# A fused convolution and gated feed-forward kernel: mask, diagonal, first weight slice and casts rearranged in its first microseconds

## The chip, the cores and the metric

The kernel runs on one core of a Trainium2 chip. The metric is the device time of one execution in microseconds (us); the median of several runs counts, lower is better. The engines are named as in the profile: PE is TensorE (PEld its weight loads), DVE is VectorE, ACT is ScalarE, POOL is GpSimd, SP is SyncE, which here only issues DMAs. A "q" behind an engine (SPq, POOLq) stands for its sequencer.

## What is computed

The input `x` has 8 sequences of 4096 tokens with 192 channels. Two steps follow each other. The first is a causal convolution of 7 taps along the sequence, one tap vector for each of 8 heads of 24 channels, with the taps normalised by a softmax. The second is a feed-forward network of 1536 hidden units whose value branch is multiplied by the rectified gate branch.

```python
w = exp(weight - max(weight, axis=-1)); w = w / (sum(w, axis=-1) + 1e-9)        # 8 heads x 7 taps
out[b, s, h, g] = sum_k w[h, k] * x_pad[b, s + k, h, g]                          # 6 zero tokens ahead
gate = maximum(out @ w_gate, 0); val = out @ w_val                               # 192 -> 1536
result = (gate * val) @ w_out                                                    # 1536 -> 192
```

All inputs and the output are float32; the kernel computes its matmuls in float16, summed in float32.

## The kernel before, in words

**Streams and units.** The 8 sequences are treated as two streams of four sequences: stream 0 (sequences 0 to 3) lies on partitions 0 to 63 and stream 1 (4 to 7) on partitions 64 to 127. A unit is 1024 tokens of both streams, 16 units in all, each in two windows of 512 tokens. The 192 channels are three chunks `c` of 64.

**Dense work.** `gate_val` (L528) runs for each window over 12 blocks `f` of 128 hidden units. Each `f` has 6 matmuls for the gate and 6 for the value (L541: three chunks, two streams, 64 rows each), then ScalarE applies the rectifier (L552) and VectorE the product (L553). Two PSUM tiles `ps` are taken for each `f` out of four, so the value tile of `f` comes free for `f + 2` when VectorE has made its product. `half_pass` (L570) projects back to 192 channels. In the first window, blocks f=0 and f=1 are treated stream by stream, and ahead of f=5 `second_block` (L394) computes the convolution of the second 512 tokens.

**The convolution.** From unit 1 on, VectorE, ScalarE and GpSimd compute the convolution of the next unit beside the dense work ("lanes"), from transposed tokens `x_r` and the tap columns `tap`. The first tokens can't wait for that, so TensorE convolves them: `conv_dense` (L352, matmul L377) multiplies token tiles `x_h` with band matrices, one for each head, which hold that head's 7 taps on diagonals. In `first_block` (L387) each of the three chunks has 40 such matmuls: 16 for the tiles `jj` = 1 to 4 of stream 0, 16 for those of stream 1 and 8 for tile `jj` = 0 (the first rows of both streams) in chunk 0; chunks 1 and 2 go tile by tile. A cast moves each chunk's result to `xc` (L392; ScalarE for c=0 and 2, VectorE for c=1).

**The start.** The order of the work is written out by hand (`manual_schedule`): each engine takes its instructions in program order. The start contains:
- the taps `wr` (L101) and, on SP's queue, stream 0's tokens as float32 into `stage`, a view of the buffer `prods` (L122), then the first rows of both streams (L138), behind a memset of their zero padding (L137);
- on GpSimd's queue a memset of `spaced` (L126), stream 1's tokens straight into `x_h` as float16 (L127), then the mask (`affine_select`, L128), which puts ones on the diagonals of `spaced`;
- the weight slices (`load_w`, L170), cut at the columns in `CUTS`: a slice's 64 rows of each chunk go to partitions 0 to 63, and `both_halves` (L177) copies them to partitions 64 to 127, on VectorE for slices 0 and 1 and on GpSimd (`pool_halves`) for the rest;
- the softmax: largest tap (L251), exponentials `ex` on ScalarE (L254), sum (L258), reciprocal (L259), the reciprocals on a diagonal, `over` (L261); `same` and `places` are sums over the mask (L238);
- TensorE's warm-up matmuls on constants (`warm_up`, L154); the matmul L272, which spreads the normalised taps over partitions; the product `diag` (L282); 14 matmuls that build the bands (L292); the evictions of the bands (`fill_band`, L329) by VectorE and ScalarE;
- the normalised taps (L304) and ten small DMAs that spread them into `tap` (L310) for the lanes;
- ScalarE's two casts of stream 0's tokens to float16 (L317) and VectorE's cast of the first rows (L335).

## Time and profile before

| what | value |
|---|---|
| median of 3 runs | 766.02 us (765.96 to 767.08) |
| span of the profiled execution, first to last instruction | 764.4 us |
| what lies around the span, by the median | 1.6 us |
| busy: PE, DVE, ACT, POOL | 99%, 92%, 79%, 50% of the span |
| granted TensorE clock in the profile's rows | 1.00 in each stage |
| first convolution matmul (L377), first dense matmul (L541) | 5.65 us, 7.66 us after the span's start |

A timeline row reads: start in us, duration in us, engine, line of the kernel, operation, what it writes and reads, how many instructions were merged into the row, and in brackets the idle time of the engine before it and what ended it. PE's matmuls overlap, so their durations contain the way through the array. A row of the DMA view names a queue, its packets, megabytes and busy share of the 16 DMA engines in a window. A row that is an issue of a DMA ends with the size and the time from the issue to the landing.

### The profile page before, as it was taken

To read this page: it belongs to the slowest core of one execution; us is meant where nothing else is said; L and a number is where in the kernel's file an instruction comes from. 1 tells how busy PE (TensorE), PEld (TensorE's weight loads), DVE (VectorE), ACT (ScalarE), POOL (GpSimd) and SP (SyncE) were. 2 spreads that over 40 slices of the span, in tenths; PEclk is the share of its full clock that TensorE was granted. 3 is DMA by queue.
4 is the path that set the end of the run, shared out by engine and by line. 5 is a ranking of instruction groups with operands and counts; after the bars stand their busy time and mean duration, and the time that the engine had idled before them with its cause. 6 is when DMAs were issued, how large, how long until landed. Compare 5 with 4: busy or idle time off the path is not lost.

```text
span 764.4 us, 25103 instructions
## 1 busy us (share of the span) xinstructions
PE 760.3 (99%) x10929; PEld 501.3 (66%) x10929; DVE 705.6 (92%) x763; ACT 600.9 (79%) x735; POOL 378.4 (50%) x244
## 2 busy tenths in 40 slices
PE   9999999999999999999999999999999999999998
PEld 5494674947649476584855848567494674947648
DVE  7998999999999999999999999999999999999891
ACT  6787887878878887887878878787787887876571
POOL 9419448093571926729175390853909347090000
PEclk9999999999999999999999999999999999999999
DMA  9969039290452805528073271722819134220202
GB/s 123 134 102 148 7 96 81 65 111 22 95 67 83 97 23 107 49 85 94 30 112 40 85 94 44 120 16 90 89 44 125 13 97 60 66 48 15 71 1 84
DMA packets 131830, 56.00 MB, mean 73 GB/s; under 512 B 96392, under 2 KB 131720, under 8 KB 131720
## 3 DMA queue, kind: packets, MB, share of 16 engines
q1 hardware_dynamic: 90680, 38.81, 23.9%
q0 software_dynamic: 40896, 15.50, 20.3%
q8 instruction: 85, 1.39, 0.8%
q14 instruction: 25, 0.20, 0.1%
q10 hardware_dynamic: 144, 0.10, 0.0%
HBM read 31.48 MB, written 25.17 MB: 74 GB/s over the span
## 4 chain that ended last, share of the span: by engine, by line
PE 99%; DVE 0%; ACT 0%; issue 0%
PE ps L541 65%; PE ps L570 32%; PE ps L619 1%; PE ps L377 0%; PE ps L154 0%; PE ps L411 0%; DVE band L329 0%; PE ps L272 0%; ACT acc L596 0%; PE ps L292 0%
## 5 line engine op out<-in xcount | busy, mean ns | idle before, releaser
L553 DVE TENSOR_TENSOR hT<-gr,ps 128x1024 f16<-128x1024 f16 (+1 forms) x386 | 469.0, 1216 | 36.6 <-ACT gr L552 9.4
L552 ACT ACTIVATE gr<-ps 128x1024 f16<-128x1024 f32 (+1 forms) x386 | 392.9, 1019 | 101.9 <-PE ps L541 99.7
L491 POOL TENSOR_TENSOR prods<-prods 128x1344 f32<-128x1344 f32 x70 | 212.4, 3034 | 290.0 <-DVE prods L487 286.7
L541 PE MATMUL ps<-xc,Wg 64*128 64x512 f16 x2304 | 311.9, 376 | 0.0
L541 PE MATMUL ps<-xc,Wv 64*128 64x512 f16 x2304 | 311.9, 376 | 0.0
L570 PEld LDWEIGHTS <-hT 64*128 64x128 f16 x5952 | 245.9, 94 | 3.7
L570 PE MATMUL ps<-Wo,hT 64*128 64x192 f16 x5952 | 248.1, 243 | 0.0
L541 PEld LDWEIGHTS <-Wv 64*128 64x128 f16 x2304 | 129.8, 94 | 118.5 <-DVE hT L553 0.3
L541 PEld LDWEIGHTS <-Wg 64*128 64x128 f16 x2304 | 112.3, 94 | 132.8 <-issue 0.2
L515 DVE SCALAR_TENSOR_TENSOR acc<-x_r,tap,acc 128x576 f32<-128x576 f16 x225 | 165.3, 813 | 0.0
L485 ACT ACTIVATE prods<-x_r,tap 128x448 f32<-128x448 f16 x222 | 130.1, 660 | 0.0
L596 ACT COPY out_s<-ps 128x768 f32<-128x768 f32 (+1 forms) x64 | 45.5, 711 | 51.3 <-PE ps L570 40.0
L203 POOL DMA_DIRECT2D x_e<-in_x_dram x58 | 47.0, 823 | 16.6 <-ACT acc L501 12.8
L465 POOL COPY x_p<-x_e 128x960 f16<-128x960 f16 (+1 forms) x58 | 50.3, 906 | 1.2 <-DMA x_e<-in_x_dram 1.1
L491 POOL TENSOR_TENSOR xc<-prods 128x1344 f16<-128x1344 f32 x14 | 42.4, 3029 | 1.1
L515 DVE SCALAR_TENSOR_TENSOR xc<-x_r,tap,acc 128x576 f16<-128x576 f16 x45 | 34.1, 813 | 0.0
L501 ACT ACTIVATE acc<-x_r,tap 128x576 f32<-128x576 f16 x45 | 31.4, 763 | 0.0
L487 DVE TENSOR_SCALAR prods<-x_r,tap 128x448 f32<-128x448 f16 x70 | 26.6, 450 | 0.0
L596 DVE COPY out_s<-ps 128x384 f32<-128x384 f32 (+1 forms) x16 | 8.7, 541 | 11.9 <-PE ps L619 9.4
L619 PE MATMUL ps<-Wo,hT 128*128 128x192 f16 x96 | 8.1, 246 | 0.0
L619 PEld LDWEIGHTS <-hT 128*128 128x128 f16 x96 | 7.9, 98 | 0.2 <-issue 0.2
L154 PE MATMUL ps<-const-bfloat16-1.0 128*128 128x512 bf16 (+1 forms) x9 | 3.9, 572 | 0.8 <-PEq L719 0.8
(54 smaller groups left out, 56.3 us busy)
## 6 DMA issues: line engine op xcount, KB each, us to landing
out_dram<-out_s SPq DMA_DIRECT2D x62, 384.0 KB, 2.7
x_e<-in_x_dram POOLq DMA_DIRECT2D x34, 192.0 KB, 7.4
x_e<-in_x_dram POOLq DMA_DIRECT2D x24, 240.0 KB, 5.6
x_r<-x_p SPq DMA_TRANSPOSE x131, 5.1
Wo<-in_moe_w_out_dram POOLq DMA_DIRECT2D x1, 576.0 KB, 7.3
x_h<-in_x_dram POOLq DMA_DIRECT2D x2, 210.0 KB, 4.8
Wg<-in_moe_w_gate_dram POOLq DMA_DIRECT2D x4, 96.0 KB, 4.1
Wv<-in_moe_w_val_dram POOLq DMA_DIRECT2D x4, 96.0 KB, 4.0
```

What stands on the lines that cost most here:

```text
L203: first = nc.gpsimd.dma_start(out=xe[:, j0 + start : j0 + n, st, :, :].rearrange("p j c r -> p j (c r)"), in_=bass.AP(tensor=x.tensor, off ...
L465: nc.gpsimd.tensor_copy(out=xp[:, j0 : j0 + n, :, st, :], in_=xe[:, j0 : j0 + n, st, :, :])
L485: engine.activation(out=out, in_=in_, func=ACTF.Copy, scale=scale)
L487: engine.tensor_scalar(out=out, in0=in_, scalar1=scale, scalar2=None, op0=ALU.mult)
L491: nc.gpsimd.tensor_tensor(out=pr[:, 0] if k < KW - 1 else xc[v + 1][:, :, LDVE:UNIT], in0=pr[:, 0], in1=pr[:, k], op=ALU.add,)
L501: nc.scalar.activation(out=accs[v][:, c, :], in_=shifted(v, c, 0, 0), func=ACTF.Copy, scale=tap[:, c, 0:1],)
L515: nc.vector.scalar_tensor_tensor(out=xc[v][:, c, 0:LDVE] if k == KW - 1 else acc[:, c, :], in0=shifted(v, c, k, 0), scalar=tap[:, c, k : k ...
L541: nc.tensor.matmul(out=pss[i][:, st, :], lhsT=W[64 * st : 64 * st + 64, c, 128 * f : 128 * (f + 1)], rhs=xcb[64 * st : 64 * st + 64, c, WI ...
L552: nc.scalar.activation(out=gr[:, sts], in_=pss[0][:, sts], func=ACTF.Relu)
L553: nc.vector.tensor_tensor(out=h[:, f, sts], in0=gr[:, sts], in1=pss[1][:, sts], op=ALU.mult)
L570: mm = nc.tensor.matmul(out=outs[q], lhsT=h[64 * r : 64 * r + 64, f, st, 128 * q : 128 * (q + 1)], rhs=Wo[64 * r : 64 * r + 64, f, :], sta ...
L596: one(out=dst[:, step * j : step * j + step], in_=src[:, step * j : step * j + step])
```

## The change

- The mask (`affine_select`) is filled ahead of GpSimd's first DMA issue, which loads stream 1.
- The memset and the transfer of the first rows move from ahead of the warm-up to behind the largest-tap reduction.
- The diagonal of reciprocals is made in two operations instead of three. `ex` gets one more row. It holds 2^127 beside the diagonal and 0 on it, so that a sum over taps for each of 8 columns is the softmax's sum on the diagonal and huge elsewhere; its reciprocal is then `over`. The row is filled from the mask ahead of the largest-tap reduction, and `same` moves there too. The sum `sm`, its reciprocal and the normalised taps for `tap` are now made by VectorE behind its last band, with the ten small DMAs behind them.
- The last warm-up matmul of the first seven (256 columns) goes.
- The weight slices are cut every 256 columns, so slice 0 has 256 columns instead of 128 and serves f=0 and f=1. VectorE copies its first 128 columns where it copied slice 0, and the second 128 behind the first block, ahead of slice 1.
- The cast of stream 0's tokens is shared: ScalarE casts channels 0 to 63 of all four tiles and channels 64 to 191 of tiles 1 and 2; GpSimd casts these channels of tiles 3 and 4, between its weight issues.
- In the first block VectorE takes the cast of chunk 2 instead of chunk 1.

```diff
     nc.gpsimd.memset(spaced[:], 0.0)
-    nc.gpsimd.dma_start(out=xts[0][0:SUB, 1:GSUB, 1, :], in_=body(1))
     nc.gpsimd.affine_select(
...
     )
-    nc.vector.memset(stage(0, 32, 0, 2, 0, 1), 0.0)
-    nc.sync.dma_start(
-        out=stage(PAD, FIRST, 0, 2, 0, 1),
...
-    )
+    nc.gpsimd.dma_start(out=xts[0][0:SUB, 1:GSUB, 1, :], in_=body(1))
...
-    warm_up(512, 512, 512, 512, 512, 512, 256)
+    warm_up(512, 512, 512, 512, 512, 512)
...
-    CUTS = [0, 128, 384, 640, 896, 1152, DFF]
+    CUTS = [0, 256, 512, 768, 1024, 1280, DFF]
...
-    def both_halves(copy, s, dst):
-        cols = slice(CUTS[s], CUTS[s + 1])
+    def both_halves(copy, s, dst, half=None):
+        lo, hi = CUTS[s], CUTS[s + 1]
+        cols = slice(lo, hi) if half is None else slice(lo + 128 * half, lo + 128 * half + 128)
         copy(out=dst[64:128, :, cols], in_=dst[0:64, :, cols])
...
+    def cast_x(copy, j0, j1, cols):
+        copy(
+            out=xts[0][0:ROWS0, j0:j1, 0, cols],
+            in_=stage(0, ROWS0, 0, 1, j0, j1 - j0)[:, :, cols],
+        )
+
     load_w(0)
-    load_w(1)
+    load_w(1, 1)
+    cast_x(nc.gpsimd.tensor_copy, 3, 5, slice(64, D))
+    load_w(1, 2)
     load_w(2)
...
-    ex = const.tile([H, KW + 1, SEG], FP)
+    ex = const.tile([H, KW + 2, SEG], FP)
...
+    FAR = 2.0**127
+    nc.vector.tensor_scalar(
+        out=ex[:, KW + 1, 0:H],
+        in0=spaced[0:H, 0, GAP : GAP + H],
+        scalar1=-FAR,
+        scalar2=FAR,
+        op0=ALU.mult,
+        op1=ALU.add,
+    )
+    same = const.tile([SUB, SEG], FP)
+    summed(same[:], pitch_k, SEG, GAP)
     mx = const.tile([H, 1], FP)
     nc.vector.tensor_reduce(
         out=mx[:], in_=wr[:], axis=mybir.AxisListType.X, op=ALU.max, negate=True
     )
+    nc.vector.memset(stage(0, 32, 0, 2, 0, 1), 0.0)
+    nc.sync.dma_start(
+        out=stage(PAD, FIRST, 0, 2, 0, 1),
...
+    )
     nc.scalar.activation(
         ex[:, 0:KW, :], wr[:].unsqueeze(2).to_broadcast([H, KW, SEG]), ACTF.Exp, bias=mx[:]
     )
-    sm = const.tile([H, 1], FP)
-    nc.vector.tensor_reduce(out=sm[:], in_=ex[:, :, 0], axis=mybir.AxisListType.X, op=ALU.add)
-    nc.vector.reciprocal(sm[:], sm[:])
     over = const.tile([H, H], FP)
-    nc.vector.tensor_scalar(
+    nc.vector.tensor_reduce(
         out=over[:],
-        in0=spaced[0:H, 0, GAP : GAP + H],
-        scalar1=sm[:],
-        scalar2=None,
-        op0=ALU.mult,
-    )
-    same = const.tile([SUB, SEG], FP)
-    summed(same[:], pitch_k, SEG, GAP)
+        in_=ex[:, :, 0:H].rearrange("h k j -> h j k"),
+        axis=mybir.AxisListType.X,
+        op=ALU.add,
+    )
+    nc.vector.reciprocal(over[:], over[:])
     summed(places[:, SUB - SEG : SUB - SEG + SEG + KW - 1], pitch_k - 1, SEG + KW - 1, GAP)
...
-    taps = const.tile([H, KW], FP)
-    nc.scalar.activation(taps[:], ex[:, 0:KW, 0], ACTF.Copy, scale=sm[:])
     tap = const.tile([128, NCH, KW], FP)
...
-    for cols in (slice(0, 64), slice(64, D)):
-        nc.scalar.copy(
-            out=xts[0][0:ROWS0, 1:GSUB, 0, cols],
-            in_=stage(0, ROWS0, 0, 1, 1, GSUB - 1)[:, :, cols],
-        )
+    cast_x(nc.scalar.copy, 1, 5, slice(0, 64))
+    cast_x(nc.scalar.copy, 1, 3, slice(64, D))
...
     fill_band(0, [3], nc.vector.tensor_copy)
+    taps = const.tile([H, KW], FP)
+    sm = const.tile([H, 1], FP)
+    nc.vector.tensor_reduce(
+        out=sm[:], in_=ex[:, 0 : KW + 1, 0], axis=mybir.AxisListType.X, op=ALU.add
+    )
+    nc.vector.reciprocal(sm[:], sm[:])
+    nc.vector.tensor_scalar(
+        out=taps[:], in0=ex[:, 0:KW, 0], scalar1=sm[:], scalar2=None, op0=ALU.mult
+    )
...
-            both_halves(nc.vector.tensor_copy, 0, Wg)
-            both_halves(nc.vector.tensor_copy, 0, Wv)
+            both_halves(nc.vector.tensor_copy, 0, Wg, 0)
+            both_halves(nc.vector.tensor_copy, 0, Wv, 0)
...
-            copy = nc.vector.tensor_copy if c == 1 else nc.scalar.copy
+            copy = nc.vector.tensor_copy if c == 2 else nc.scalar.copy
...
     first_block()
+    both_halves(nc.vector.tensor_copy, 0, Wg, 1)
+    both_halves(nc.vector.tensor_copy, 0, Wv, 1)
     both_halves(nc.vector.tensor_copy, 1, Wg)
     both_halves(nc.vector.tensor_copy, 1, Wv)
```

22 lines of the change are left out of this document (11 added, 11 removed).

## The prediction, made before the result was known

> **What bounds the kernel now.** I read four things in this order: the page's head, the chain of waits, a table of busy time by stage, and the timeline of each engine over the first 16 us. The page first.
>
> ```profile
> span 764.4 us, 25103 instructions
> ...
> PE ps L541 65%; PE ps L570 32%; PE ps L619 1%; PE ps L377 0%; PE ps L154 0%; PE ps L411 0%; DVE band L329 0%; PE ps L272 0%; ACT acc L596 0%; PE ps L292 0%
> ```
>
> The chain that ended last is TensorE's gate and value matmuls (L541, 65%) and its projection (L570, 32%). The 384 rounds of f (16 units, two halves, 12 f) thus take 0.65 x 764.4 / 384 = 1.29 us each. The table by stage shows TensorE (the third number) from the first dense matmul (7.66 us) on: 753.70 us busy of 756.74. The other 3 us are mostly the tail, in which results leave.
>
> ```profile
> 7.66:764.40 756.74, 753.70 (x10788) 497.48 (x10784) 701.06 (x747) 596.76 (x726) 371.75 (x230) 1.00 0.45 73
> ```
>
> So nothing behind the start can be won or hidden: a delay of TensorE in the first microseconds moves the end by as much, and the change is worth what it does to the start. The chain of the first 8 us:
>
> ```profile
> 0.85 2.93 PE ps L154 x7
> ...
> 4.79 0.27 PE ps L292 x7
> ...
> 5.65 2.08 PE ps L377 x106
> ```
>
> Warm-up matmuls, the spread of the taps (L272), the bands (L292), VectorE's eviction of the bands, then the convolution (L377), then the dense work. The chain names no transfer, but the waits of TensorE's weight loads do:
>
> ```profile
> 5.58 0.45 PEld L377 LDWEIGHTS <-x_h 110*32 110x32 f16 x16 [0.42 <-ACT x_h L317]
> 6.18 1.38 PEld L377 LDWEIGHTS <-x_h 110*32 110x32 f16 x104 [0.15 <-DMA x_h<-in_x_dram]
> 10.96 0.33 PEld L541 LDWEIGHTS <-Wv 64*128 64x128 f16 x6 [0.34 <-DVE hT L553]
> ```
>
> Three places decide. At 5.58 the convolution waits for ScalarE's cast, which waits for stream 0. At 6.18 it waits for the DMA of stream 1. At 10.96 the third block f=2 waits for VectorE's product of f=0, which frees its PSUM tile; the matmuls still in the array cover that wait only just, so a longer one is TensorE's loss. VectorE's rows:
>
> ```profile
> 2.79 0.15 DVE L258 TENSOR_REDUCE sm<-ex 8x1 f32<-8x8 f32 x1 [0.45 <-ACT ex L254]
> 2.98 0.15 DVE L259 RECIPROCAL sm<-sm 8x1 f32<-8x1 f32 x1
> 3.25 0.22 DVE L261 TENSOR_SCALAR over<-spaced,sm 8x8 f32<-8x8 f32 x1
> 3.39 0.35 DVE L238 TENSOR_REDUCE same<-spaced 112x16 f32<-112x112 f32 x1
> ...
> 5.67 0.36 DVE L335 CAST x_h<-prods 102x384 f16<-102x384 f32 x1
> 5.95 0.27 DVE L329 CAST band<-ps 128x112 f16<-128x112 f32 x1
> 6.49 0.28 DVE L177 COPY Wg<-Wg 64x384 f16<-64x384 f16 x1 [0.27 <-DMA Wg<-in_moe_w_gate_dram]
> 6.75 0.58 DVE L177 COPY Wv<-Wv 64x384 f16<-64x384 f16 x1
> 7.36 0.69 DVE L392 CAST xc<-ps 128x512 f16<-128x512 f32 x1
> 8.08 0.42 DVE L177 COPY Wg<-Wg 64x768 f16<-64x768 f16 x1
> 8.43 0.53 DVE L177 COPY Wv<-Wv 64x768 f16<-64x768 f16 x1
> ```
>
> ```profile
> 9.62 1.28 DVE L553 TENSOR_TENSOR hT<-gr,ps 128x512 f16<-128x512 f16 x2 [0.67 <-ACT gr L552]
> ```
>
> VectorE is done with its copies at 8.43 + 0.53 = 8.96 and idles 0.67 us until ScalarE's first result. That is the whole reserve in front of the products; what the change puts there beyond it, TensorE waits for.
>
> **The change, part by part.**
>
> *The chain to the bands.* Sum, reciprocal and product (from 2.79 to 3.25 + 0.22 = 3.47) become a sum of 64 terms and a reciprocal of 64 values. Neither is in the trace. The lower bound of each is its small row, 0.15 for 8 terms or fewer; the upper is L238's, 0.35 for 112. On the line between them 64 elements take 0.15 + 56 x 0.20/104 = 0.26, and I take that for both: the second ends near 2.79 + 0.26 + 0.26 = 3.31 instead of 3.47, so L272 starts some 0.15 us sooner (bounds 0.3 sooner, 0.05 later), and the 256-column warm-up no longer stands in its way. `same` (0.35) and the mask's new row move ahead of the largest-tap reduction, where VectorE waits for the taps' transfer in any case. They need the mask, which now comes early enough (below); if it came 0.2 us later, this chain would lose as much.
>
> How much of it reaches TensorE's convolution? Hardly any. The next bound is ScalarE's first cast, which starts when stream 0 lands:
>
> ```profile
> 5.12 0.41 ACT L317 CAST x_h<-prods 110x256 f16<-110x256 f32 x1 [1.60 <-DMA prods<-in_x_dram]
> ...
> 7.93 0.58 ACT L392 CAST xc<-ps 128x512 f16<-128x512 f32 x1 [0.49 <-PE ps L377]
> ```
>
> That cast is the same instruction after the change, so the convolution begins at 5.58 instead of 5.65: 0.07 won, and even this ends at the wait for stream 1.
>
> A rule speaks against the shorter chain too. The rows: the first seven L154 matmuls take 2.93 us for 3328 columns, 0.45 per 512, and seven of L292 then take 0.27 for 448, or 0.31 per 512, so the array sped up near 4.8, almost 4 us after its first matmul. The Trainium skill, "TensorE: Matmul & The Clock Gate", Part 1, says that the full clock comes after a busy window of about 3.4 us that runs freely and does not follow the kernel. By it the bands, brought forward 0.15, would run further into the slow time, and less than half of the 0.15 would remain; by the rows alone all of it. The sum is the same either way, as stream 0 hides both.
>
> *Stream 1, behind the mask.* GpSimd's rows:
>
> ```profile
> 0.81 0.33 POOL L126 MEMSET spaced<- 112x280 f32 x1 [0.29 <-POOLq L719]
> 1.42 0.88 POOL L127 DMA_DIRECT2D x_h<-in_x_dram  x1 [0.28 <-issue]
> 2.39 0.36 POOL L128 TENSOR_SCALAR_AFFINE_SELECT spaced<-ones 112x112 f32<-112x112 f32 x1
> 2.67 0.68 POOL L170 DMA_DIRECT2D Wg<-in_moe_w_gate_dram  x1
> ...
> 4.59 0.63 POOL L170 DMA_DIRECT2D Wv<-in_moe_w_val_dram  x1
> ```
>
> The mask (0.36) now starts near 1.2 instead of 2.39, and the issue of stream 1 slips from 1.42 to between 1.5 (the next issue followed the mask's start by 0.28) and 1.9 (a full 0.36 plus the 0.28 gap that stood behind the memset). But the transfer did not run when it was issued:
>
> ```profile
> q1 hardware_dynamic: 248, 0.18, 110.2%
> q1 hardware_dynamic: 151, 0.10, 89.5%
> q0 software_dynamic: 54, 0.02, 34.2%
> ```
>
> These are the queues (SP's is q1, GpSimd's q0; packets, MB, share) at 3.5 to 4.0 and, the two last rows, at 4.0 to 4.5: GpSimd's queue moved nothing until SP's load was nearly through. A slip of 0.1 to 0.4 is therefore mostly covered, and the first rows, which went ahead of stream 1, may now go beside or behind it. Bounds for its landing: 0.24 earlier (then the convolution runs through from 5.58 without the stop at 6.18) to 0.45 later. I take no change: the convolution ends 0.05 earlier at most.
>
> *The first rows' transfer.*
>
> ```profile
> 1.67 0.48 SPq L138 DMA_DIRECT2D prods<-in_x_dram  x1
> prods<-in_x_dram SPq DMA_DIRECT2D x1, 144.0 KB, 4.0
> ```
>
> It landed at 1.67 + 4.0 = 5.67, just when VectorE took it. Its memset now stands behind the largest-tap reduction, just ahead of the sum at 2.79, so it is issued near 2.8, 1.1 us later. Landing between 5.67 (it waited in SP's queue behind stream 0 anyway) and 2.8 + 4.0 = 6.8. I take 5.75, since stream 0 fills SP's queue until about 4. Behind it on VectorE stand its cast (0.36), the last band of half 0 (0.27) and now the sum, reciprocal and product of the taps (from 2.79 to 3.47: up to 0.68), so the first weight copies begin near 6.9. The taps' ten small DMAs move with that product; what they bring is used only by the lanes, well behind the start.
>
> *Casts shared.* ScalarE's second cast halves; GpSimd takes the other part, queued behind three weight issues, and waits there for stream 0 to near 5.1. All issues behind it move back by some 0.9 us: the Wv slice for f=2 from 4.59 to 5.5, then the second block's input and the further slices. But with 256-column cuts the slices behind the first two are used one f (1.29) later, which covers 0.9. So nothing for this; without that cover it would cost up to 0.9.
>
> *Weights of f=0.* Wg and Wv of slice 0 are twice as large. They were used at 6.49 and 6.75. From 6.0 to 6.5 GpSimd's queue moved
>
> ```profile
> q0 software_dynamic: 210, 0.09, 142.7%
> ```
>
> so 48 KB more in each cost 0.27 us if bytes count and nothing if packets do (their number stays). Half of it gives 6.65 and 7.05, ahead of VectorE's turn. Its copies of the first halves take 0.84 as a pair (6.49 to 7.33) and end at 6.9 + 0.84 = 7.74, about as TensorE arrives (7.66 before). The value matmuls come second, so I take nothing, with no reserve (0.3 at the upper bound).
>
> *VectorE ahead of its products.* Here is the cost. The cast of chunk c=2, not c=1, is now VectorE's: it starts at 7.93 - 0.05 = 7.88 and ends at 8.57 (0.69; ScalarE took 0.58). Behind it stand four copies, not two: the second halves of slice 0 (a pair as at 6.49 to 7.33, 0.84) and slice 1 (a pair as at 8.08 to 8.96, 0.88). High end 1.72. Low end, if the second of each pair is as quick as the first (the starts lie 0.26 and 0.35 apart): 1.22. I take 1.47, one of the two slow ones. The two products (1.28) then run from 8.57 + 1.47 = 10.04 to 11.32, and the weight load of 10.96 follows at about 11.38.
>
> **Sum: 0.42 us later**, from 10.96 to 11.38; all behind it is TensorE at work. The span becomes 764.8. The runs' median (766.02) lies 1.6 above the span of the one profiled, so the forecast is 766.4.
>
> **Rivals.**
>
> *Stream 1 lands early* because the first rows no longer run ahead, and the copies are quick. The convolution ends 0.29 sooner, the casts and copies (1.22) are done near 9.5, and the products start when ScalarE's result comes. TensorE is as early as before or 0.05 better: 766.0. For it: GpSimd's queue stood idle until 4.0. Against: its issue is later.
>
> *The mask does push stream 1 back*, by up to 0.45, which is the opposite of what the reordering needs: the 0.42 becomes 0.85 and the time 766.9. It decides as soon as TensorE's weight load of stream 1 starts behind 6.2.
>
> *The first rows become the last thing to land* (the slower side). It decides from a landing past about 5.8. At 6.8, as its own row gives with the new issue: cast and band end at 7.43, the convolution's second chunk starts 1.0 late, the taps' three operations end at 8.1, the pair of copies at 8.95, the cast of c=2 at 9.65, four copies at their long price at 11.37, the products at 12.65: 1.7 us late, 767.7.
>
> *The array's clock rises later* since a matmul of its warm-up is gone. The convolution's 2.08 us hold 0.2 of waiting; at half speed the rest costs 1.9 more, and if the clock rises half-way, 0.95: 767.4. Against: L272 takes the freed time at once, so the array is no more idle.
>
> *GpSimd's mask is slow on first use.* The trace starts it 0.09 behind the issue before it (1.42 + 0.88 = 2.30, start 2.39). If something was prepared unseen beside that issue, it took at most from the memset's end to the mask's start, 2.39 - 1.14 = 1.25; stream 1 would wait for that, some 1.3 us on top of the 0.42: 767.7. The Trainium skill, "GPSIMD Engine Reference", § 2.1 (Instruction dispatch), names a load of about 6 us for the first call of a freshly loaded routine; by that the time would be near 772, and the trace's 0.09 disagrees with it here.
>
> **How the numbers follow.** Chances: forecast 0.46, stream 1 early 0.22, mask pushes 0.16, first rows last 0.10, clock 0.04, slow mask 0.02. Measurements of this kernel tell about 0.2% (1.5 us) from no change. The forecast's own range, by the copies' two ends and stream 1 unchanged, is 766.1 to 766.7. The range from 765.7 to 767.4 takes in the early and pushed stream with a little noise of the runs (765.96 to 767.08), and leaves out the last three rivals. To be faster by over 1.5 us a fifth of the start would have to vanish: 0.04, from the tail of the early stream. Slower by over 1.5 us: 0.13, most of the last three rivals.
>
> **What would show it.** Right: a wait of TensorE's weight load for VectorE's product near 11.4, VectorE without idle time between its c=2 cast and the first product, the convolution's start near 5.6. Wrong: the wait before f=2 gone; a wait for the first rows' cast or for a band inside the convolution; the convolution's second stream starting well off 6.2; weight copies that wait for their DMA.

## The result and the profile after

| | kernel before | kernel after |
|---|---|---|
| median of 7 runs each | 766.09 us (765.96 to 767.82) | 769.61 us (767.74 to 770.53) |
| span of the profiled execution | 764.4 us | 768.5 us |

The ratio is 1.0038 (95% interval 1.0027 to 1.005). By the medians the kernel is 3.5 us slower, 3.2 more than forecast (766.4) and 2.2 outside the range. The seven runs of the kernel after fall in two groups, 767.74 to 768.13 and 769.61 to 770.53; both have to be explained, and the profiled execution belongs to the second.

The page after, its head and its chain:

```profile
span 768.5 us, 25104 instructions
...
PE 99%; DMA 1%; POOL 0%; issue 0%; ACT 0%; POOLq 0%
PE ps L560 65%; PE ps L589 32%; PE ps L638 1%; DMA x_h<-in_x_dram 1%; PE ps L396 1%; PE ps L430 0%; POOL spaced L126 0%; POOL spaced L127 0%; ACT acc L615 0%; POOLq L740 0%
```

The chain now names a transfer, which it did not before: stream 1 into `x_h`. The same chain for the first 16 us, in order of time (start, duration, what):

```profile
0.81 0.34 POOL spaced L126
1.15 0.07 issue
1.22 0.32 POOL spaced L127
1.54 0.25 issue
1.79 5.71 DMA x_h<-in_x_dram
7.50 0.04 issue
7.54 2.75 PE ps L396 x95
10.29 5.87 PE ps L560 x37
```

The warm-up, the taps and the bands are gone from it. In their place stand the memset, the mask (L127), the issue at 1.79, and 5.71 us until stream 1 has landed. The timeline of TensorE and its weight loads:

```profile
5.77 0.88 PE L396 MATMUL ps<-band,x_h 110*32 110x104 f16 x16
7.54 2.75 PE L396 MATMUL ps<-band,x_h 110*32 110x104 f16 x104 [0.90 <-DMA x_h<-in_x_dram]
7.54 2.51 PEld L396 LDWEIGHTS <-x_h 110*32 110x32 f16 x104 [1.14 <-DMA x_h<-in_x_dram]
10.22 0.61 PE L560 MATMUL ps<-xc,Wg 64*128 64x512 f16 x2
...
12.76 1.25 PE L560 MATMUL ps<-xc,Wg 64*128 64x512 f16 x6
13.84 0.81 PE L560 MATMUL ps<-xc,Wv 64*128 64x512 f16 x6
```

Two things went wrong. The weight load of stream 1, at 6.18 before, starts at 7.54: 1.36 us later. And the 104 matmuls behind it then take 2.75 us, where the whole convolution took 2.08. One line of the kernel asked by itself shows the reason in its minimum, median and maximum duration; first the kernel before, then the kernel after:

```profile
L377 PE MATMUL ps<-band,x_h x120: 203/209/220, 5.6 to 7.5; 110*32 110x104 f16 x48, 110*24 110x104 f16 x16, 110*16 110x104 f16 x16, 110*8 110x104 f16 x16
```

```profile
L396 PE MATMUL ps<-band,x_h x120: 245/291/291, 5.8 to 10.0; 110*32 110x104 f16 x48, 110*24 110x104 f16 x16, 110*16 110x104 f16 x16, 110*8 110x104 f16 x16
```

The median of the same matmul went from 209 to 291 ns. The row of the kernel after also holds the 16 matmuls ahead of the wait (the first starts at 5.8), and its shortest is 245: the array was slow already before it waited for stream 1. The 14 matmuls that build the bands tell the same, before and after:

```profile
L292 PE MATMUL ps<-diag,places x14: 193/193/240, 4.6 to 5.1; 112*128 112x64 f16 x14
```

```profile
L307 PE MATMUL ps<-diag,places x14: 212/241/241, 4.5 to 5.2; 112*128 112x64 f16 x14
```

In the kernel before the array comes up to speed among them; in the kernel after it does not, and the wait for stream 1 finds it still slow. The dense matmuls, grouped by line and form from 9 to 14 us (count, busy us, mean ns), before and after:

```profile
L541 PE MATMUL ps<-xc,Wv 64*128 64x512 f16 x24 | 3.4, 377 | 0.0
```

```profile
L560 PE MATMUL ps<-xc,Wv 64*128 64x512 f16 x8 | 2.3, 567 | 0.0
```

A third as many value matmuls got done. The table by stage (window, PE's busy time and count, granted clock, DMA share, GB/s) says nothing of it. In the kernel after the granted clock stands at 1.00:

```profile
10.00:12.50 2.50, 2.50 (x22) 1.00 1.57 191
```

This 1.00 is no measurement. The trace's record of the granted clock begins only where the full clock was granted, 4.78 us behind the span's start in the kernel before and 13.63 in the kernel after. Ahead of its first entry the table shows 1.00 for want of one, and so it did in the first stages of the kernel before. The durations and starts say the same. The six matmuls that begin at 12.76 take 1.08 until the next group at 13.84. In the kernel before six take 0.65, in this one the groups of two ahead of them 0.43, or 1.29 for six. With x us at the slow pace, x/1.29 + (1.08 - x)/0.65 = 1 gives x = 0.87: the array came up to speed near 13.6, where the record begins. The kernel before at the same places:

```profile
9.64 0.83 PE L541 MATMUL ps<-xc,Wv 64*128 64x512 f16 x6
...
10.97 0.82 PE L541 MATMUL ps<-xc,Wv 64*128 64x512 f16 x6
```

The value matmuls of f=1 come at 13.84 after and at 9.64 before, 4.2 later, and the spans differ by 4.1: all of it arises ahead of this point, 1.36 by stream 1 and 2.8 by the slow array.

### The profile page after: what moved, and what is told of

Read it like the earlier page. It is cut to its first block, busy times and chain, and to the rows that moved or that the text cites. A ratio compares the mean times of both kernels' runs of the same rounds, so it can differ in the third digit from the quotient of the medians.

```text
span 768.5 us, 25104 instructions
## 1 busy us (share of the span) xinstructions
PE 763.7 (99%) x10928; PEld 514.9 (67%) x10928; DVE 707.3 (92%) x768; ACT 600.8 (78%) x734; POOL 378.3 (49%) x245
## 4 chain that ended last, share of the span: by engine, by line
PE 99%; DMA 1%; POOL 0%; issue 0%; ACT 0%; POOLq 0%
PE ps L560 65%; PE ps L589 32%; PE ps L638 1%; DMA x_h<-in_x_dram 1%; PE ps L396 1%; PE ps L430 0%; POOL spaced L126 0%; POOL spaced L127 0%; ACT acc L615 0%; POOLq L740 0%
## 5 line engine op out<-in xcount | busy, mean ns | idle before, releaser
L560 PE MATMUL ps<-xc,Wg 64*128 64x512 f16 x2304 | 315.6, 377 | 0.0
L560 PE MATMUL ps<-xc,Wv 64*128 64x512 f16 x2304 | 315.2, 377 | 0.0
L560 PEld LDWEIGHTS <-Wv 64*128 64x128 f16 x2304 | 134.1, 94 | 115.1 <-issue 0.8
L560 PEld LDWEIGHTS <-Wg 64*128 64x128 f16 x2304 | 119.9, 94 | 125.9 <-issue 1.5
L396 PE MATMUL ps<-band,x_h 110*32 110x104 f16 (+7 forms) x240 | 5.2, 248 | 0.9 <-DMA x_h<-in_x_dram 0.9
```

What stands on the lines that cost most here:

```text
L560: nc.tensor.matmul(out=pss[i][:, st, :], lhsT=W[64 * st : 64 * st + 64, c, 128 * f : 128 * (f + 1)], rhs=xcb[64 * st : 64 * st + 64, c, WI ...
```

## The experiments

All times are medians beside runs of the kernel before on the same chip (765.96 to 766.04 in every group). "Before + x" means the kernel before with x alone changed.

### The two moved transfers

**Before + the mask ahead of GpSimd's first issue.**

```diff
-    nc.gpsimd.dma_start(out=xts[0][0:SUB, 1:GSUB, 1, :], in_=body(1))
     nc.gpsimd.affine_select(
...
     )
+    nc.gpsimd.dma_start(out=xts[0][0:SUB, 1:GSUB, 1, :], in_=body(1))
```

> The kernel before with one edit: the mask ahead of GpSimd's first issue. Issue theory (stream 1 is late because its issue slipped by 0.37 us): TensorE's weight load for stream 1 starts near 7.5 us instead of 6.18, and the time is 767.5 or more. Rows theory (it is late because the first rows' transfer no longer goes ahead of it): the load starts at 6.55 at the latest and the time is within 0.4 us of before.

766.81 against 766.01, ratio 1.0011 [1.0002, 1.0021]. Its timeline:

```profile
1.22 0.32 POOL L127 TENSOR_SCALAR_AFFINE_SELECT spaced<-ones 112x112 f32<-112x112 f32 x1
1.79 0.92 POOL L136 DMA_DIRECT2D x_h<-in_x_dram  x1 [0.25 <-issue]
...
7.09 1.38 PEld L377 LDWEIGHTS <-x_h 110*32 110x32 f16 x104 [0.79 <-DMA x_h<-in_x_dram]
```

The issue slipped by 0.37 (1.42 to 1.79), stream 1 by 0.91 (6.18 to 7.09). Stream 1 lies between what my two theories had (6.55 at the latest, or near 7.5), and a slip costs more than itself. The DMA view from 4.5 to 5.0 us shows where, first the kernel before, then this one (packets, MB, share):

```profile
q0 software_dynamic: 214, 0.08, 136.3%
```

```profile
q0 software_dynamic: 60, 0.02, 97.2%
```

In the half microsecond in which GpSimd's queue moved 214 packets before, it now moves 60, and each occupies its engine for 0.972 x 16 x 500 / 60 = 130 ns instead of 51. From 5.0 to 5.5 they take 63 ns, but there are 120 of them where there were 288. SP's queue moved nothing from 4.5 to 5.5, so it is not the other queue that slows them.

**Before + the first rows' memset and transfer behind the largest-tap reduction.**

```diff
-    nc.vector.memset(stage(0, 32, 0, 2, 0, 1), 0.0)
-    nc.sync.dma_start(
-        out=stage(PAD, FIRST, 0, 2, 0, 1),
...
     nc.vector.tensor_reduce(
         out=mx[:], in_=wr[:], axis=mybir.AxisListType.X, op=ALU.max, negate=True
     )
+    nc.vector.memset(stage(0, 32, 0, 2, 0, 1), 0.0)
+    nc.sync.dma_start(
+        out=stage(PAD, FIRST, 0, 2, 0, 1),
...
```

> The kernel before with one edit: the memset and the transfer of the first rows behind the largest-tap reduction. Rows theory: the first rows and stream 1 share the DMA engines and both land late, stream 1's weight load starts near 7.5 us and the first rows' cast near 7.2, time 767.5 to 770. Issue theory: stream 1's weight load stays near 6.2 or sooner, the first rows' cast starts between 5.7 and 6.8, time 766 to 767.

766.67 against 766.01, 1.001 [1.0001, 1.0018]. The convolution now runs through both streams and stops for the first rows:

```profile
6.39 0.36 DVE L335 CAST x_h<-prods 102x384 f16<-102x384 f32 x1 [0.77 <-DMA prods<-in_x_dram]
...
6.80 1.23 PEld L377 LDWEIGHTS <-x_h 102*32 102x32 f16 x88 [0.55 <-DVE x_h L335]
```

VectorE takes them 0.7 later than before (5.67), and TensorE's weight load waits 0.55. Stream 1 isn't late here; from 4.0 to 4.5 us GpSimd's queue moved

```profile
q0 software_dynamic: 252, 0.10, 160.6%
```

where it had moved 54 before. With the first rows out of its way it starts sooner, as my rival of an early stream 1 had it; but the convolution then waits for the first rows.

**Before + both moved.** The two diffs above together.

> The kernel before with both steps moved at once, the mask ahead of GpSimd's first issue and the first rows' transfer behind the largest-tap reduction, and nothing else of the change. Alone the first cost 0.80 us and the second 0.66. If the two delays add, because stream 1 and the first rows share the DMA engines, the time is 766.0 + 1.46 = 767.5, near the quick runs of the kernel after (767.74) less the 0.31 of the weight slices: 767.43. If they overlap, because each is a wait of the same stretch of the convolution, it is the larger one alone: 766.8 to 766.9. If the array's slow speed then strikes as it did in the kernel after, with the idle stretch ahead of stream 1 near 0.9 us and the 256-column warm-up still there, some runs lie 2 us higher, near 769.5.

767.36 against 765.96, 1.0018 [1.0009, 1.0027]; +1.40 where +0.80 and +0.66 add to 1.46. So by the medians the delays add. Two of the 11 runs lie at 768.5 and above. In the timeline of a quicker one, stream 1 is later than with the mask alone, since the first rows now run beside it:

```profile
7.26 1.47 PEld L377 LDWEIGHTS <-x_h 110*32 110x32 f16 x104 [1.29 <-DMA x_h<-in_x_dram]
...
8.81 0.39 PE L541 MATMUL ps<-xc,Wg 64*128 64x512 f16 x2
```

The dense work begins at 8.81 instead of 7.66: 1.15 of the 1.40. TensorE itself stood idle for 1.13 us ahead of stream 1, longer than the 0.90 of the kernel after, and still its matmuls on both sides of that wait are quick. The record of the clock begins at 4.27 here, ahead of the wait:

```profile
L377 PE MATMUL ps<-band,x_h x120: 203/209/220, 5.6 to 8.7; 110*32 110x104 f16 x48, 110*24 110x104 f16 x16, 110*16 110x104 f16 x16, 110*8 110x104 f16 x16
```

**The kernel after + the first rows early again.** The second diff reversed.

> The changed kernel with the first rows' memset and transfer back in their old place. Rows theory: stream 1's weight load is back at 6.5 us or sooner, the array's clock rises near 4.8 us as before, time 766.1 to 766.7 (the original forecast). Issue theory: the load stays near 7.5 us and the time at 768 to 770.

768.62 (767.85 to 769.25), 1.003 [1.0021, 1.0038]; five runs at 767.85 to 768.09 and six at 768.62 to 769.25. The timeline is of a run of the first group:

```profile
7.08 1.38 PEld L396 LDWEIGHTS <-x_h 110*32 110x32 f16 x104 [1.27 <-DMA x_h<-in_x_dram]
8.56 0.39 PE L560 MATMUL ps<-xc,Wg 64*128 64x512 f16 x2
```

Stream 1 comes as late as with the mask alone; the first rows by themselves can't carry the loss.

**Is it the mask, or only the time of the issue?** Before + the memset of `spaced` three times, the mask left behind the issue:

```diff
     nc.gpsimd.memset(spaced[:], 0.0)
+    nc.gpsimd.memset(spaced[:], 0.0)
+    nc.gpsimd.memset(spaced[:], 0.0)
     nc.gpsimd.dma_start(out=xts[0][0:SUB, 1:GSUB, 1, :], in_=body(1))
```

> The kernel before with GpSimd's memset done three times ahead of the issue of stream 1 (twice did not move the issue), the mask behind it: the issue should slip to about 1.8 us, as with the mask first. Slip theory: TensorE's weight load of stream 1 near 7.1 us, its packets slow at first, time 766.8. Mask theory: weight load at 6.55 at the latest, time 766.0 to 766.4.

766.75 against 766.00, 1.0011 [1.0002, 1.0019]. In the timeline:

```profile
1.86 0.88 POOL L129 DMA_DIRECT2D x_h<-in_x_dram  x1
...
6.89 1.38 PEld L379 LDWEIGHTS <-x_h 110*32 110x32 f16 x104 [0.96 <-DMA x_h<-in_x_dram]
```

No mask stands ahead of the issue, and the loss is the same: 0.75 here, 0.80 there. It is the time of the issue. The slow packets are here as well: 32 packets at a share of 48.4% from 4.5 to 5.0 us, 121 ns each.

Three smaller steps towards that were no tests, since they hardly moved the issue. With the memset behind the issue it started at 1.40, with a second memset at 1.47, with half a memset more at 1.45 (1.42 before):

> The kernel before with the opposite edit: GpSimd's issue of stream 1 ahead of the memset of the mask's tile, 0.55 us sooner. Issue theory: TensorE's weight load of stream 1 follows stream 0's matmuls without the stop at 6.18 us, the convolution ends some 0.2 us sooner, time 765.6 to 765.9. Rival (the first rows' cast or a band binds at once): 766.0, no change.

> The kernel before with GpSimd's memset of the mask's tile done twice ahead of the issue of stream 1, the mask itself behind it as before: the issue slips by the same 0.35 us without the mask. Slip theory (only the time of the issue counts): TensorE's weight load of stream 1 starts near 7.1 us as with the mask first, time 766.8. Mask theory (the mask's own operation ahead of the issue is what hurts): the load at 6.55 at the latest, time 766.0 to 766.4.

> The kernel before with a smaller additional memset (120 of 280 columns) ahead of the issue: a slip of about half as much. If the landing moves in proportion (0.9 us for 0.37): weight load of stream 1 near 6.6, time 766.4. If there is a step: 6.2 to 6.35 (766.0) or 7.1 (766.8).

766.04, 766.11 and 766.07, ratios 1.0006 [0.9996, 1.0015], 1.0004 [0.9995, 1.0013] and 1.0001 [0.9992, 1.001].

**Are the packets slow because their rows are touched for the first time?** Before + mask first + a small early transfer on SP's queue that reads 16 of stream 1's rows into a tile of its own.

```diff
     nc.sync.dma_start(out=stage(0, SUB, 0, 1, 1, GSUB - 1), in_=body(0))
+    touched = const.tile([16, D], FP)
+    nc.sync.dma_start(
+        out=touched[:],
...
+            tensor=x.tensor, offset=x.offset + (NB * S + FIRST) * D, ap=[[26 * D, 16], [1, D]]
...
```

> The kernel before with the mask first, and in addition a small DMA on SP's queue, right behind stream 0's, that reads 16 rows spread over stream 1's tokens into a spare tile. First-touch theory (stream 1's packets are slow at first because nothing has read that memory yet): the slow packets go, weight load of stream 1 near 6.4, time 766.1 to 766.3. Otherwise: slow packets as with the mask first, weight load near 7.1, 766.8.

767.84, 1.0025 [1.0016, 1.0033]; stream 1 at 7.37 instead of 7.09. The extra transfer made the time worse. The packets from 4.5 to 5.0 us, though, are quicker, 62 ns each in place of 130, and more of them move than with the mask alone (60):

```profile
q0 software_dynamic: 101, 0.04, 78.9%
```

So this does not settle the question: quicker first packets did not bring stream 1 sooner, and SP's queue moved 16 packets beside them. Why the packets are slow stays open.

### The slow array

**The kernel after + constant matmuls in the gap.** Three warm-up matmuls of 512 columns between the two streams of chunk 0, and the 256-column one back. This adds work on constants whose result nobody reads.

```diff
-    warm_up(512, 512, 512, 512, 512, 512)
+    warm_up(512, 512, 512, 512, 512, 512, 256)
...
         for jj, sts in both:
+            if g == 0 and c == 0 and sts == (1,) and jj == late[0]:
+                warm_up(512, 512, 512)
```

> The changed kernel with constant matmuls added: the 256-column one restored, and three of 512 columns between the first chunk's matmuls for stream 0 and for stream 1, where TensorE stood idle for 0.9 us. Clock theory (the idle gap keeps the array at half speed until 13.6 us): stream 1's weight load still starts near 7.5 us, but the dense matmuls run at full pace from the start, time 767.4 to 768. Without the clock's part: no gain, 769.6 or more.

768.54 (768.06 to 768.75), 1.0028 [1.0017, 1.0039]. None of its 7 runs lies near 770. In the timeline of one stream 1 comes at 7.33, hardly sooner than in the kernel after, but the array is at full pace:

```profile
7.33 1.54 PE L398 MATMUL ps<-band,x_h 110*32 110x104 f16 x104
8.80 0.39 PE L562 MATMUL ps<-xc,Wg 64*128 64x512 f16 x2
...
12.73 0.82 PE L562 MATMUL ps<-xc,Wv 64*128 64x512 f16 x6 [0.52 <-DVE hT L574]
```

In this run the record of the clock begins at 6.37, just ahead of the three constant matmuls (6.57). So the timeline does not show them at work; what speaks for them is the 7 times.

**The kernel after + only the 256-column matmul.**

```diff
-    warm_up(512, 512, 512, 512, 512, 512)
+    warm_up(512, 512, 512, 512, 512, 512, 256)
```

> The changed kernel with only the 256-column warm-up matmul restored; the idle gap ahead of stream 1 stays. Warm-up theory: the runs gather at 767.7 to 768.3, none near 770. Gap theory: they scatter from 767.7 to 770.5 as without it, median 769 to 770.

769.48 (768.03 to 770.36), 1.0039 [1.0027, 1.0052]: nothing won, 4 of 6 runs in the later group. With the kernel after (4 of 7) that is 8 of 13. Had the filled gap the same share, none of 7 would be a chance of (5/13)^7, about 1 in 800.

**Before without that matmul.**

```diff
-    warm_up(512, 512, 512, 512, 512, 512, 256)
+    warm_up(512, 512, 512, 512, 512, 512)
```

> The kernel before without the 256-column warm-up matmul, all else kept. Warm-up theory (the array's clock needs that matmul): more of the runs lie at 767 and above than of the kernel before, median 766.5 to 768. Gap theory (only an idle TensorE behind 5.2 us holds the clock down, and here there is none): 766.0, the same spread as before.

765.94 against 765.98, 0.9999 [0.9991, 1.0008]. By the median the removed warm-up matmul costs nothing by itself. Two of the 12 runs lie at 767.8, and the profiled one is of these.

**Before without the two single warm-up matmuls** that stand between L272, the bands and the convolution. No transfer moves.

```diff
-    warm_up(512)
...
-    warm_up(512)
```

> The kernel before without the two single 512-column warm-up matmuls (behind L272 and behind the bands): no transfer and no other engine's work changes, TensorE only idles more between 3.8 and 5.6 us. Clock theory: in more than half of the runs the array's clock rises a whole step later (near 8 to 10 us), those runs lie at 767.5 to 768.5, median 767 to 768. Rival (these matmuls do nothing for the clock): 766.0 with before's spread.

767.16 against 766.04, 1.0014 [1.0005, 1.0022]; 10 of 11 runs are 0.8 to 1.8 us late. Its timeline:

```profile
5.76 3.08 PE L375 MATMUL ps<-band,x_h 110*32 110x104 f16 x120 [0.23 <-ACT x_h L315]
8.77 0.61 PE L539 MATMUL ps<-xc,Wg 64*128 64x512 f16 x2
```

Every input is there, and yet the convolution takes 3.08 instead of 2.08 and the first dense pair 0.61 instead of 0.39. Less work of TensorE ahead of the convolution is enough for a slow array.

**When the clock rises.** The start of the trace's record of the granted clock, in us behind the span's start, and TensorE's idle time ahead of stream 1, each from one profiled run:

```
                                    full clock from   idle ahead of stream 1
kernel before                             4.78        none
before + both moved                       4.27        1.13
after + first rows early                  4.39        1.11
after + gap filled                        6.37        filled
before without the two singles            9.49        none
after, both orders undone                 9.84        none
before without the 256-column matmul     10.23        none
after + the 256-column matmul            13.38        0.43
kernel after                             13.63        0.90
```

All 20 profiled runs lie in three groups: 15 from 4.04 to 6.37, three from 9.49 to 10.23, two from 13.38 to 13.63. A wait behind the rise leaves the clock alone (second and third row). A late rise comes without the wait too: 4 of 11 runs with both orders undone lie at 768.7 or more, and 5 of 11 with stream 1's issue ahead of the memset at 767.6 or more, where 9 of 155 runs of the kernel before have a span above 765.5. So a run can miss its first rise without the wait. In the two profiles that have both, the rise is put off further, from near 10 to near 13.5. That the wait does this is argued from these two profiles and from the 7 runs with the gap filled; why a run misses the first rise is open.

### VectorE ahead of its products

**Before + the weight slices of 256 columns and VectorE's cast of c=2.**

```diff
-    CUTS = [0, 128, 384, 640, 896, 1152, DFF]
+    CUTS = [0, 256, 512, 768, 1024, 1280, DFF]
...
-            copy = nc.vector.tensor_copy if c == 1 else nc.scalar.copy
+            copy = nc.vector.tensor_copy if c == 2 else nc.scalar.copy
...
     first_block()
+    both_halves(nc.vector.tensor_copy, 0, Wg, 1)
+    both_halves(nc.vector.tensor_copy, 0, Wv, 1)
```

> The kernel before with two edits of the change: slices of 256 columns with VectorE's two additional copies ahead of the products, and VectorE casting chunk 2 instead of chunk 1. VectorE theory (the prediction's sum): the value weight load of f=2 waits for VectorE until about 11.4 us instead of 10.96, time 766.4, between 766.2 and 766.7. Rival (the reserve of 0.67 us and earlier data cover it): 766.0.

766.29 against 765.98, 1.0004 [0.9995, 1.0012]. The interval by itself doesn't tell this from no change; the timeline does:

```profile
7.89 0.69 DVE L393 CAST xc<-ps 128x512 f16<-128x512 f32 x1 [0.31 <-PE ps L378]
...
9.52 0.40 DVE L178 COPY Wv<-Wv 64x768 f16<-64x768 f16 x1
9.95 3.66 DVE L554 TENSOR_TENSOR hT<-gr,ps 128x512 f16<-128x512 f16 x5
...
11.38 0.82 PE L542 MATMUL ps<-xc,Wv 64*128 64x512 f16 x6 [0.20 <-DVE hT L554]
```

VectorE goes from its last copy to the product without a pause, and the value matmuls of f=2 start at 11.38 instead of 10.97, waiting for that product. The span of its quick runs is 764.6 against 764.3, so 0.3 of the 0.41 reach the end. The weight copies of f=0 wait for their DMA here (6.67 and 7.29, where 6.65 and 7.05 were forecast), without a cost: the dense work begins at 7.67.

### What else the change holds

**The kernel after with both moved steps undone.**

```diff
+    nc.gpsimd.dma_start(out=xts[0][0:SUB, 1:GSUB, 1, :], in_=body(1))
     nc.gpsimd.affine_select(
...
-    nc.gpsimd.dma_start(out=xts[0][0:SUB, 1:GSUB, 1, :], in_=body(1))
     spare = const.tile([H, 1], FP)
```

and the first rows' memset and transfer back ahead of `spare`, the row of 2^127 behind the largest-tap reduction and `same` behind the reciprocals.

> The changed kernel with both moved steps back in place: stream 1's issue ahead of the mask and the first rows' transfer early; the operations that read the mask follow the exponentials. Slices of 256, the chunk 2 cast, the shared cast, the diagonal in two operations and the shorter warm-up stay. VectorE theory: stream 1's weight load near 6.2, the value weight load of f=2 near 11.4, time 766.2 to 766.7. Rival (the shared cast's delay of GpSimd's queue or the weights' landing costs as well): 767 or more.

766.45 against 766.04, 1.0012 [1.0001, 1.0022]; four of the 11 runs lie at 768.7 to 768.9, the profiled one among them. The median is the 766.4 of my prediction, but not for its reason. Each run also has a span. The medians of time and span, and of what lies outside the span:

```
                                         time     span    outside the span
kernel before, 155 runs in 6 groups   765.96-766.04  764.2-764.3   1.70-1.73
slices and cast of c=2 alone           766.29    764.6    1.69
both orders undone                     766.45    764.4    2.03
kernel after                           769.61    767.6    2.03
```

With the orders undone, the span grew by 0.1 only; 0.3 of the 0.4 lie outside it. I counted what lies around the span as a constant. Three more kernels take the rest apart.

**Before + diagonal, taps on VectorE and shared casts, without the 256-column matmul;** orders and slices as before.

> The kernel before with the reciprocals' diagonal in two operations, the tap weights computed on VectorE behind the bands, the first casts shared with GpSimd and no 256-column warm-up; both moved steps and the weight slices as before. My prediction costs this at nothing to 0.07 won: 765.95 to 766.05. If the later taps on VectorE or the cast on GpSimd cost something, it is the 0.45 of the kernel with the orders undone (766.45) less the 0.31 of the slices: 766.15. If the shorter chain to the bands were worth its whole 0.15, 765.85.

766.39 against 765.96, 1.0009 [1.0, 1.0018]; outside the span 2.05. The span of the profiled execution is 764.1. In its timeline:

```profile
5.49 1.80 PEld L395 LDWEIGHTS <-x_h 110*32 110x32 f16 x120 [0.24 <-ACT x_h L222]
7.38 0.39 PE L559 MATMUL ps<-xc,Wg 64*128 64x512 f16 x2
```

The convolution runs through without the stop at 6.18, and the dense work begins 0.28 sooner (7.38 against 7.66). In the spans no gain is shown: their median is 764.4, and three of the 11 lie at 765.9 to 766.1. The 0.28 is that of one execution.

**Before + only the seven tap weights on VectorE,** scaled behind the last band instead of on ScalarE ahead of its casts, with their ten small DMAs.

```diff
-    nc.scalar.activation(taps[:], ex[:, 0:KW, 0], ACTF.Copy, scale=sm[:])
...
     fill_band(0, [3], nc.vector.tensor_copy)
+    nc.vector.tensor_scalar(
+        out=taps[:], in0=ex[:, 0:KW, 0], scalar1=sm[:], scalar2=None, op0=ALU.mult
+    )
```

> The kernel before with only one thing changed: the seven tap weights of the eight lanes are scaled on VectorE behind the last band of half 0, not on ScalarE ahead of its first casts. Every run has a span and a time; the difference, what lies outside the profiled span, is 1.70 to 1.73 (median) in the kernel before and in each kernel with the old tap code, and 2.03 to 2.05 in each kernel with the rewritten tap code, the kernel after among them. If the tap weights' move makes that difference, this kernel has 2.0 outside its span, and its time is 766.3 with an unchanged span of 764.2 to 764.3. If it does not, the difference stays 1.7 and the time 766.0 (0.1 more if VectorE's extra 0.22 ahead of the first weight copies reaches TensorE).

766.25 against 765.99, 1.0004 [0.9995, 1.0013]; span 764.2 (before 764.3), outside the span 2.03. The interval of the time alone would allow no change. The time less the span does not: it is 1.97 to 2.05 in every run. So this move, of one operation and its ten DMAs, makes the 0.31.

**Before + only the shared casts.**

```diff
-    for cols in (slice(0, 64), slice(64, D)):
-        nc.scalar.copy(
...
+    cast_x(nc.scalar.copy, 1, 5, slice(0, 64))
+    cast_x(nc.scalar.copy, 1, 3, slice(64, D))
...
-    load_w(1)
+    load_w(1, 1)
+    cast_x(nc.gpsimd.tensor_copy, 3, 5, slice(64, D))
+    load_w(1, 2)
```

> The kernel before with only the first casts shared: GpSimd takes half of ScalarE's second cast, behind its third issue of weights. My prediction costs this at nothing: 766.0. If it is this part that lengthens what lies outside the span from 1.7 to 2.0, the time is 766.3 with an unchanged span of 764.2 to 764.3. If neither this kernel nor the one with the taps on VectorE shows it, the reciprocals' diagonal is left as its cause.

766.00 against 765.99, 0.9999 [0.999, 1.0008], outside the span 1.73: nothing.

No version was quicker than the kernel before by more than the runs can tell.

## Why the prediction was wrong

Two steps failed: that a later issue of stream 1 is mostly covered, and that the array comes up to speed as it did in the kernel before.

**The account.** The quick group of the kernel after (767.74 to 768.13) is 1.65 to 2.04 above 766.09. Outside the span lie 0.31 of it (2.03 less 1.72); inside, the spans of that group (765.7, 766.0 and 766.1) are 1.4 to 1.8 above 764.3. That group has no profile, so I read its nearest neighbours (spans 766.0 and 766.1). The late transfers make 0.90 to 1.14 of it: the first dense matmul at 8.56 with the first rows early again, and at 8.80 with the gap filled, against 7.66. VectorE makes the rest: from the first dense matmul to the value matmuls of f=2 it is 12.73 - 8.80 = 3.93 with the gap filled, against 10.97 - 7.66 = 3.31 before. Its last copy takes 0.91 there, beside GpSimd's own two copies (10.12 to 11.83); with the slices and the cast alone, where it is done as GpSimd's begin, it takes 0.40. The median, 769.61, lies 1.5 to 1.9 above the quick group; that is the slow array.

**Stream 1, the step that failed.** "A slip of 0.1 to 0.4 is therefore mostly covered ... I take no change", with 0.45 as the upper bound of its landing. The slip was within what I gave (0.37), and I had the point from which the rival decides ("as soon as TensorE's weight load of stream 1 starts behind 6.2"). Its price was wrong: I carried the slip over one to one at most, since GpSimd's queue moved nothing until SP's load was nearly through. That reading holds for an issue at 1.42 (252 packets in place of 54, once the first rows are out of the way). With the later issue SP's queue is empty and GpSimd's moves few and slow packets. TensorE's weight load follows the issue by 6.18 - 1.42 = 4.76 us in the kernel before, by 6.89 - 1.86 = 5.03 with three memsets, by 7.09 - 1.79 = 5.30 behind the mask, and by 7.54 - 1.79 = 5.75 in the kernel after, where the first rows run beside it.

**The first rows.** I took 5.75 for their landing and 6.8 as its bound. Alone they came at 6.39, inside the bounds and past the 5.8 from which I let the rival decide; I chose the wrong end. With both transfers moved VectorE took them at 6.78, and in the kernel after later than the bound. The timeline of VectorE after:

```profile
2.98 0.26 DVE L278 TENSOR_REDUCE over<-ex 8x8 f32<-8x72 f32 x1
3.28 0.19 DVE L284 RECIPROCAL over<-over 8x8 f32<-8x8 f32 x1
...
7.19 0.64 DVE L335 CAST x_h<-prods 102x384 f16<-102x384 f32 x1 [1.61 <-DMA prods<-in_x_dram]
...
12.61 0.40 DVE L171 COPY Wv<-Wv 64x768 f16<-64x768 f16 x1
13.21 1.28 DVE L572 TENSOR_TENSOR hT<-gr,ps 128x512 f16<-128x512 f16 x2 [0.20 <-ACT gr L571]
```

I kept the two moves apart, each with its own reason to be covered, and never put the price of both together.

**The array's clock.** I gave it 0.04, a price of 0.95 to 1.9, and argued only about the removed matmul: "L272 takes the freed time at once, so the array is no more idle". By the median that part holds (the kernel before without it: 765.94). Here the failed step is that I took the clock of the kernel before as given, with a rise near 4.8, and did not ask what a run costs in which it has not risen when stream 1 makes TensorE wait. In the profiled run it rose at 13.63, and the slow pace made 2.8 us. Less work ahead of the convolution makes the rise late (the kernel without the two single matmuls), and with the gap filled none of 7 runs is in the last group. The Trainium skill, "TensorE: Matmul & The Clock Gate", Part 1, says that the speed is judged in free-running windows of about 3.4 us, and that the time of the change varies from run to run. By that, an estimate: the window in which the gap of 0.90 fell is lost, and the next whole one after 7.54 ends between 7.54 + 3.4 and 7.54 + 6.8, at 10.9 to 14.3. The trace agrees with 13.63, and in the 20 profiled runs the entry of the full clock lasts 761.172, 757.759 or 754.345 us, in steps of 3.413; the start of it differs from run to run, from 4.04 to 13.63. The same page of the Trainium skill also calls the ramp less than 1% of a typical span; here its 1.5 to 1.9 us are some 0.2%, and about half of what the change moved.

**The chain to the bands.** Two operations of 0.26 each were predicted; the rows above have 0.26 and 0.19. In the kernel after the 14 matmuls of the bands start at 4.50 instead of 4.63, close to the 0.15 forecast, but the bands are no earlier (5.07 against 5.09): at the slow pace these matmuls take 0.91 where they took 0.62. That "stream 0 hides both" was half right: by themselves (the kernel with the diagonal and the casts) these parts let the dense work begin 0.28 sooner in the one execution that was profiled, where I had 0.07.

**VectorE's products: right.** 10.96 to 11.38 was forecast and 11.38 measured, alone. In the kernel after the wait is not there, which I had named as a sign against it. It isn't one: the slow array comes later than the product. With the array at full pace the wait is back (0.52 of it in the row at 12.73), and larger, since the last copy took 0.91 there. I had priced the four copies at 1.47 without asking what GpSimd does beside them: with the slices and the cast alone they take 1.31 (8.61 to 9.92), with the gap filled 1.64 (9.63 to 11.27).

**Casts and the weights of f=0.** Casts: nothing, as predicted. The weights of f=0 landed later (7.29 for the second with the slices and the cast alone) and cost nothing there, as I took it. **The mask on first use:** it took 0.32 and began 0.08 behind the memset (0.81 + 0.33 = 1.14 to 1.22). The 6 us that the Trainium skill, "GPSIMD Engine Reference", § 2.1, names for a first call are not seen here.

**What lies around the span.** I took 1.6 as it was; moving the seven tap weights adds 0.31.

**Open.** Why the later issue makes few and slow packets. Why a run misses the first rise of the clock, and whether the 8 of 13 late runs with the gap are more than the 4 of 11 with both orders undone. And what the move of the tap weights does outside the span.

## What to carry to other kernels

A step of 0.3 us put ahead of a queue's first transfer need not be worth 0.3 us: here a second memset cost nothing and the mask 0.8. Price the landing, not the issue, and with all transfers that the change moves at once. Where a wait of TensorE grows within the first microseconds, ask whether the array has come up to speed by then; if not, add to the price that it may run at half pace for several more. Look for it in the durations of equal matmuls, not in the table's granted clock. Compare time less span between versions: a part can cost something that no view of the profile shows.

## What the runs showed of the hardware that was not expected

- The first transfer of GpSimd's queue was there 4.76 us behind an issue at 1.42, and 5.03 to 5.30 behind one at 1.79 to 1.86. In the later ones the packets from 4.5 to 5.0 took 121 to 130 ns each in place of 51.
- The issue was not had sooner: with nothing ahead of it on GpSimd it still started at 1.40, and a second memset of 0.33 moved it only to 1.47.

```profile
1.40 0.88 POOL L126 DMA_DIRECT2D x_h<-in_x_dram  x1 [0.88 <-POOLq L719]
```

- The array came up to speed at 4.04 to 6.37 us in 15 of 20 profiled runs, at 9.49 to 10.23 in three and at 13.38 to 13.63 in the two with a wait for stream 1 ahead of the rise. Once up, it kept its pace through waits of 1.11 and 1.13 us. Of the kernel before, 9 of 155 runs have a span above 765.5; none of these was profiled.
- One and the same copy of VectorE (64x768) took 0.40 us by itself and 0.91 beside GpSimd's copies.
- Seven values scaled on VectorE instead of ScalarE, with their ten small DMAs behind, put 0.31 us outside the profiled span, in every run.
